# Tiny loads at the start of an attention and mixture-of-experts kernel, pair 1's loads, and a remade instruction order

## Chip, cores and metric

One core of one Trainium2 chip. The metric is the device time of one execution in microseconds (us); the median of three timed runs before the change is 482.71 us (482.61 to 484.01).

## What is computed

Attention of 4 batches with 8 heads, 768 positions and head size 64, in which each query sees the first 4 keys (the sinks) and the last 128; its output, 3072 tokens of 512 numbers, then goes through a mixture of 8 experts, of which each token takes one.

```python
keep = is_sink | in_window                      # window 128, 4 sinks
scores = where(keep, scale * q @ kT, -1e9)
a = softmax(scores); x = a @ v                  # x: 3072 tokens x 512
e_idx = argmax(x @ w_gate)                      # one expert for each token
eom = sigmoid(x @ w_output_gate)
for e in range(8):                              # tokens of expert e
    out[mask] = gate_w * eom[mask, e] * (relu(x[mask] @ w1[e]) @ w2[e])
```

## The kernel before

*Stages.* Attention goes through 16 pairs of heads (`pair(p)`). A pair loads q and k (for two heads), v for two pairs at once, and for each batch the sink values. Its scores come in three tiles of PSUM (L1481, `score(j)`, f32); DVE masks a tile and takes the row maximum (L1490 to L1497, `fold`), ACT scales the maxima (L1509) and takes the exponentials (L1502). PE transposes them (L1530), ACT copies them out (L1533), GpSimd (POOL) masks them (L568), and PE multiplies them by v in six steps, av0 to av5 (L1597), and by the sink values (L1621). The result is transposed, normed and written to DRAM (`xd`). After each four pairs tokens are routed to experts on DVE. Then 18 slots follow, each for one expert and up to 384 of its tokens: tokens are gathered, the expert's weights (4 MB) are loaded and most are split into a high and a low part (ACT L1150, DVE L1154), and PE runs two matrix products (L1299 and L1338; small slots L1312, L1245, L1260), with a ReLU between whose residue DVE makes (L1214). The scaled result is scattered to the output (L1193). The first four slots (`early`) are mixed into the last part of attention.

*The order.* Nothing here is in the order of the source. Every step is given to a `Plan` with `pl.op(engine, took, fn, r=, w=, at=, busy=, size=, behind=)`: what it reads and writes, the planned duration, how long it holds its engine, the bytes of a transfer (`size`), and other steps after which it comes (`behind`). `order()` then plays the program: at each turn it looks on each engine for the step that could start first, may take instead one that could start within a small margin (`NEAR`, for PE `AT["near"]`) and has a lower due time `at`, and takes the earliest of all engines. The due time is a priority and holds nothing back. `PIN` overwrites the due time of every step by its number. A transfer ends in the plan when all planned bytes before it and its own have passed at `RATE` (KB per us, in thousands), plus `LAND` ns; a step `behind` a transfer on its own engine waits in the plan for that planned landing. `behind` makes no wait on the chip: there each engine runs its instructions in the resulting order and waits for the data that they need, and a transfer is issued when its turn comes. For PE the plan also counts the fetching of its code: after each `CHUNK` of 256 instructions the next block must be there, and one block takes `FETCH` ns.

*The start.* PE warms up with matmuls on a constant (`begin`, L1399 and L1406) and, after pair 0's first score tile, with 14 fillers (`idle(1)`, L1399), each a step of its own that fills time while nothing else is ready. Loads go to the queues of SP (`nc.sync`) and ACT. For pair 0, q's first two blocks go to SP and k's first to ACT; k's and q's second pieces go to ACT behind a step that loads the table of exponentials. `small_loads` is one step on SP with five transfers: the gate weights `wgt` (L671, 64 KB), the two scalars `nsw_i` (L673, 8 bytes to each of 128 partitions), and the zero row of `xd` in two transfers (L674: 128 pieces of 16 bytes, L675). Pair 1's q and k (L1420) stand behind that step; v (L1443) and the sink values (L1449) stand behind nothing. `scalars` is a DVE step of eight small operations on `nsw_i` (L637 to L647); `wgt` is first used by `gate` after the fourth pair, the zero row by the first gather.

Of the kernel before, what the change touches and what calls it, by code (L numbers as in the profile page):

```python
# [19 lines left out]
P = 128  # L20
B, H, S, D = 4, 8, 768, 64
# [278 lines left out]
class Plan:  # L300

    LAG = {"PE": 260, "ACT": 60, "DVE": 80, "POOL": 55, "SP": 30, "X": 0}
    NEAR = {"PE": 60, "ACT": 60, "DVE": 60, "POOL": 100, "SP": 100, "X": 0}
    SWITCH = {"four": 170}
    RATE, LAND = 0.38, 2700
    CHUNK, FETCH = 256, 4600

    def __init__(self):
# [1649 lines left out]
```

## Time and profile before

| | before |
|---|---|
| timed runs, median (lowest to highest) | 482.71 us (482.61 to 484.01) |
| the profiled execution, its time | 486.86 us |
| its span, first to last instruction | 484.9 us |
| mean granted clock of PE | 0.992 |
| PE busy | 462.9 us (95%) |
| DVE, ACT, POOL busy | 330.7, 281.1, 151.9 us |
| moved by DMA | 116.74 MB, 241 GB/s |

The profile is one execution. Engines are PE (matmuls), PEld (PE's weight loads, which overlap matmuls), DVE, ACT, POOL; SPq, ACTq and POOLq are the instructions by which SP, ACT and POOL issue DMA transfers. PE's ends are modelled, so a busy PE may still run below its peak. A waiting engine's idle time is put down to what came last, by semaphore events; "issue" means that it waited for nothing that the profile shows. The granted clock is the share of PE's full clock that the throttle allowed.

### The profile page before, as it was taken

Reading aid. Unit: us, or ns where it says so; the run is one execution under the profiler, and the core shown is the slowest. Engines: PE = TensorE matmul, PEld = TensorE weight load, DVE = VectorE, ACT = ScalarE, POOL = GpSimd, SP = SyncE. Lnnn points to the kernel's source line nnn. Section 1 sums busy time; section 2 is a strip of 40 time slices with the busy share of each in tenths; the row PEclk is TensorE's granted clock in tenths of the full one; section 3 lists DMA queues with packets and bytes.
Section 4 is the critical chain, followed back from the end, with each engine's and each line's share of the span. In section 5 each row is a group of like instructions: output and inputs, shape, how many; then the busy total and the mean of one; then the engine's idle time right before and its main releaser. Section 6 shows DMA issues by size and latency. Waiting matters only on the chain.

```text
span 484.9 us, 13381 instructions
## 1 busy us (share of the span) xinstructions
PE 462.9 (95%) x5129; PEld 379.0 (78%) x5129; DVE 330.7 (68%) x713; ACT 281.1 (58%) x779; POOL 151.9 (31%) x270
## 2 busy tenths in 40 slices
PE   8899999998889999899999999999999999999992
PEld 4688786787679879698889999888866978968571
DVE  5675789889888989999999932605557677373200
ACT  4999879987877743466566222616536665462310
POOL 6435543837652133310532110311132121100211
PEclk9999999999989999999999999999999999999998
DMA  7665764675764775587997563855898978979980
GB/s 214 225 207 166 235 183 145 207 203 162 261 198 124 230 245 175 173 248 251 323 325 262 194 230 107 296 206 198 286 405 304 303 260 291 392 259 403 402 317 14
DMA packets 63147, 116.74 MB, mean 241 GB/s; under 512 B 8283, under 2 KB 27875, under 8 KB 63075
## 3 DMA queue, kind: packets, MB, share of 16 engines
q1 hardware_dynamic: 58226, 101.00, 62.3%
q0 software_dynamic: 4416, 14.14, 8.1%
q8 instruction: 42, 0.69, 0.6%
q10 hardware_dynamic: 432, 0.67, 0.5%
q14 instruction: 31, 0.25, 0.2%
HBM read 102.61 MB, written 13.17 MB: 239 GB/s over the span
## 4 chain that ended last, share of the span: by engine, by line
PE 66%; issue 14%; DVE 7%; ACT 4%; DMA 4%; POOL 3%; POOLq 0%; SPq 0%; ACTq 0%; DVEq 0%
PE d L1299 19%; PE d L1338 19%; PE d L1597 6%; PE d L1481 5%; PE tp L1530 4%; DMA k<-in_kx_dram 3%; PE d L1312 2%; ACT e L1502 2%; PE tp L1639 2%; PE tp L1175 2%; PE d L1621 2%; POOL out_dram L1193 2%; PE d L1260 1%; PE d L1245 1%; DVE nmx L1497 1%
## 5 line engine op out<-in xcount | busy, mean ns | idle before, releaser
L1502 ACT ACTIVATE e<-d,nmx 128x132 f32<-128x132 f32 x192 | 69.4, 377 | 1.4
L1193 POOL DMA_INDIRECT out_dram<-y,idx x21 | 22.6, 1077 | 127.4 <-ACT y L1190 115.2
L1211 ACT ACTIVATE hh<-d 128x512 fp32r<-128x512 f32 (+1 forms) x36 | 23.2, 644 | 50.8 <-PE d L1299 42.8
L1214 DVE SCALAR_TENSOR_TENSOR hl<-d,hh 128x512 fp32r<-128x512 f32 (+1 forms) x36 | 26.8, 745 | 32.7 <-ACT hh L1211 32.7
L1110 POOL DMA_INDIRECT xg<-xd,idx x21 | 24.2, 1150 | 76.2 <-PE tp L1175 33.9
L1481 PE MATMUL d<-k,q 64*64 64x128 f32 (+3 forms) x1088 | 44.3, 285 | 2.4 <-DMA k<-in_kx_dram 1.9
L1481 PEld LDWEIGHTS d<-k,q 64*64 64x64 f32 x1088 | 37.3, 135 | 10.2 <-issue 5.4
L568 POOL TENSOR_SCALAR_AFFINE_SELECT g<-f 128x512 f32<-128x512 f32 (+1 forms) x48 | 27.9, 582 | 54.2 <-ACT f L1533 48.0
L1597 PE MATMUL d<-f,v 64*64 64x128 f32 (+1 forms) x768 | 42.6, 252 | 1.2 <-issue 1.1
L1190 ACT ACTIVATE y<-d,sc 128x512 f32<-128x512 f32 (+2 forms) x29 | 17.9, 636 | 44.4 <-PE d L1338 22.9
L1502 ACT ACTIVATION_READ_ACCUMULATOR e<-d,nmx 128x1 f32 x192 | 40.5, 211 | 0.0
L1495 DVE COPY_PREDICATED d<-maskf,d 128x512 f32<-128x512 int32 (+1 forms) x48 | 29.0, 604 | 16.8 <-PE d L1481 10.9
L1597 PE MATMUL d<-g,v 64*64 64x128 f32 (+1 forms) x640 | 39.0, 253 | 1.0 <-ACT tick L1612 0.6
L1597 PEld LDWEIGHTS d<-f,v 64*64 64x64 f32 x768 | 34.6, 135 | 3.0 <-issue 2.6
L1497 DVE TENSOR_REDUCE nmx<-d 128x4 f32<-128x528 f32 x48 | 33.9, 707 | 1.6
L1597 PEld LDWEIGHTS d<-g,v 64*64 64x64 f32 x640 | 29.6, 135 | 4.1 <-issue 2.4
L1530 PE MATMUL tp<-ident,e 128*128 128x128 f32 x192 | 29.4, 281 | 2.4 <-ACT hlk L1567 2.0
L1533 ACT COPY f<-tp 128x512 f32<-128x512 f32 x48 | 28.0, 597 | 5.8 <-PE tp L1530 4.1
L1348 DVE TENSOR_SCALAR hr<-d 128x512 f32<-128x512 f32 (+1 forms) x12 | 7.7, 645 | 32.5 <-PE d L1245 18.2
L568 POOL TENSOR_SCALAR_AFFINE_SELECT f<-f 128x512 f32<-128x512 f32 (+1 forms) x48 | 28.8, 601 | 3.3
L1530 PEld LDWEIGHTS tp<-ident,e 128*128 128x128 f32 x192 | 21.1, 142 | 7.5 <-ACT e L1502 2.2
L795 POOL TENSOR_TENSOR rhs<-oh,ohj 128x512 bf16<-128x512 bf16 x12 | 15.4, 1306 | 14.3 <-DVE ohj L781 14.2
(488 smaller groups left out, 1434.1 us busy)
## 6 DMA issues: line engine op xcount, KB each, us to landing
raw<-in_w_dram SPq DMA_DIRECT2D x96, 512.0 KB
v<-in_vx_dram SPq DMA_DIRECT2D x16, 384.0 KB
xd<-x SPq DMA_DIRECT2D x16, 384.0 KB
k<-in_kx_dram SPq DMA_DIRECT2D x15, 396.0 KB
q<-in_qT_dram SPq DMA_DIRECT2D x15, 384.0 KB
wa2h<-in_w_dram SPq DMA_DIRECT2D x4, 512.0 KB
wa2l<-in_w_dram SPq DMA_DIRECT2D x4, 512.0 KB
wa1h<-in_w_dram SPq DMA_DIRECT2D x3, 512.0 KB
```

Of the source, the lines that this page charges most:

```text
L568: nc.gpsimd.affine_select(out=ap, in_=ap if src is None else src, pattern=pattern, compare_op=op, fill=fill, base=base, channel_multiplier=cm)
L1193: nc.gpsimd.indirect_dma_start(out=where, out_offset=bass.IndirectOffsetOnAxis(ap=ids(), axis=0), in_=p.get(yk)[:, 0:m], in_offset=None, b ...
L1214: nc.vector.scalar_tensor_tensor(out=p.get(hl)[:, :, 0:n], in0=p.get(ps)[:, :, 0:n], scalar=0.0, in1=p.get(hh)[:, :, 0:n].bitcast(F32), op ...
L1299: nc.tensor.matmul(out=p.get(ps)[:, j, 0:cols], lhsT=a, rhs=p.get(x)[:, d, 0:cols], start=d == 0 and i == 0, stop=d == ND - 1 and i == 2)
L1338: nc.tensor.matmul(out=p.get(ys[s][0])[:, ys[s][1], :], lhsT=h[a][:, s * P:(s + 1) * P], rhs=w[b_], start=f == 0 and i == 0, stop=f == NF ...
L1481: nc.tensor.matmul(out=to, lhsT=get(q)[r, qs], rhs=get(k)[r, c:c + n], start=True, stop=True)
L1495: nc.vector.copy_predicated(out=y[:, :, D + 4:3 * D + 4].rearrange("p n (u c) -> p n u c", u=2), mask=bc(maski[:, 1, 4:CW].rearrange("p (u ...
L1497: nc.vector.tensor_reduce(out=top(), in_=z[:, :, :, D:3 * D + 4], axis=AX.X, op=ALU.max, negate=True)
L1502: nc.scalar.activation(out=get(e)[:, t, a, :], in_=by_step()[:, a, i, D:3 * D + 4], func=AF.Exp, bias=get(nmx)[:, a, t:t + 1], scale=SCALE ...
L1530: nc.tensor.transpose(out=get(tp)[:, i, :], in_=get(e)[:, 2 * j + i // 2, i % 2, 4:CW], identity=ident)
L1533: nc.scalar.copy(out=get(f)[:, two].rearrange("p t a r -> p (t a) r"), in_=get(tp))
L1597: nc.tensor.matmul(out=o, lhsT=get(v)[rows_, kt, p % 2 * P + a * D:p % 2 * P + (a + 1) * D], rhs=get((f, g)[src == "g"])[rows_, kt, a, c0: ...
```

## The change

The step of small loads becomes three, with larger planned bytes. The second piece of pair 0's q goes to SP and no longer stands behind the table load. Pair 1's q and k, the first v and all sink values stand behind that piece in the plan. The plan's RATE, LAND and `near` change, pair 0's first two score tiles and the first five fillers get longer planned times, and the fetch of a block of code takes in the plan half the time of the queued bytes more (`CROWD`). `PIN` is new throughout: none of the 1898 due times stays, and 1900 stand there now, as there are two steps more. The diff shows only the first two lines of `PIN` on each side (numbers 10 and 11 are the second pieces of k and q; before, 12 is the small loads; after, 12 to 14 are `wgt`, the scalars and the zero row).

```diff
@@ -61,239 +61,242 @@
...
-    "xm": 12029, "st": 39215, "rt": 89574, "ft": 40462, "near": 54, "fu": 40316, "fv": -6834,
+    "xm": 12029, "st": 39215, "rt": 89574, "ft": 40462, "near": 0, "fu": 40316, "fv": -6834,
...
-    0: 170375, 1: 183025, 2: 234170, 3: 207036, 4: 209173, 5: 234024, 6: -57011, 7: -2769860, 8: -63555, 9: -60420,
-    10: -196814, 11: -213168, 12: -2613934, 13: 219356, 14: -2575280, 15: -2569229, 16: -2590146, 17: -2590366, 18:
...
+    0: 284048, 1: 304551, 2: 298792, 3: 283628, 4: 288927, 5: 291515, 6: 68786, 7: -5536575, 8: -481105, 9: -468029,
+    10: -471477, 11: -5305361, 12: -5303392, 13: -5283895, 14: -5290740, 15: 121475, 16: -4524559, 17: -5299047, 18:
...
@@ -302,8 +305,8 @@
     LAG = {"PE": 260, "ACT": 60, "DVE": 80, "POOL": 55, "SP": 30, "X": 0}
     NEAR = {"PE": 60, "ACT": 60, "DVE": 60, "POOL": 100, "SP": 100, "X": 0}
     SWITCH = {"four": 170}
-    RATE, LAND = 0.38, 2700
-    CHUNK, FETCH = 256, 4600
+    RATE, LAND = 0.37, 2900
+    CHUNK, FETCH, CROWD = 256, 4600, 0.5
 
     def __init__(self):
         self.ops, self.inst, self.fam = [], {}, {}
@@ -462,7 +465,8 @@
                 for edge in range((first // self.CHUNK + 1) * self.CHUNK, issued + 1, self.CHUNK):
                     at = t + late + o["busy"] * (edge - first) / o["count"]
                     late += max(0, ready_at - at)
-                    ready_at = max(at, ready_at) + self.FETCH
+                    ready_at = max(at, ready_at)
+                    ready_at += self.FETCH + self.CROWD * max(0, dma - ready_at)
             free[e] = t + late + o["busy"]
             if o["size"]:
                 dma = max(dma, t + o["busy"]) + o["size"] / self.RATE / 1000
@@ -667,15 +671,17 @@
         def small_loads():
             q = nc.sync
 
-            def load():
-                q.dma_start(out=wgt, in_=wgo)
+            def scalars_in():
                 for j, src in enumerate((nsink, window)):
                     q.dma_start(out=nsw_i[:, j, :], in_=src.bitcast(I32).partition_broadcast(P))
+
+            def row_0():
                 q.dma_start(out=xd[0, 0:DM].rearrange("(p c) -> p c", p=P), in_=tab[:, 0, 0, 0:4])
                 q.dma_start(out=xd[0:1, DM:XP], in_=tab[0:1, 0, 0, 0:XP - DM])
-            small = pl.op("SP", 2500, load, w=["wgt", "nsw_i", "xd0"], size=64, busy=2600, at=-1000000)
+            pl.op("SP", 2500, lambda: q.dma_start(out=wgt, in_=wgo), w=["wgt"], size=65536, busy=420, at=20000)
+            pl.op("SP", 2500, scalars_in, w=["nsw_i"], size=500000, busy=880, at=25000)
+            pl.op("SP", 2500, row_0, w=["xd0"], size=300000, busy=770, at=27000)
             pl.op("DVE", 1500, scalars, r=["nsw_i"], at=30000)
-            return small
 
         def rows(b):
             return xd[1 + b * S:1 + (b + 1) * S, :].rearrange("(t p) c -> p t c", p=P)
@@ -1425,12 +1431,12 @@
                 load(k, kx, 0, 2 * CW, "ACT", (0,), -2000000)
                 warmed = [pl.op("ACT", 1600, lambda: nc.scalar.activation(out=warm, in_=warm, func=AF.Exp), at=-1999999.5, busy=1500)]
                 paced["k"] = load(k, kx, 2 * CW, KW, "ACT", (1,), -1999999, warmed)
-                paced["q"] = load(q, qT, 2 * P, S, "ACT", (1,), -1999999, warmed)
-                paced["small"] = small_loads()
+                paced["q"] = load(q, qT, 2 * P, S, "SP", (1,), -1999999)
+                small_loads()
             for name, src, n in ((q, qT, S), (k, kx, KW))[:2 * (p > 0)]:
                 if p == 2:
                     touch([(name, 0), (name, 1)], lambda name=name: get(name), zeroed, at)
-                paced[name] = load(name, src, 0, n, "SP", (0, 1), (at, "load"), [paced[name[0], p - 1] if p > 1 else paced["small"]])
+                paced[name] = load(name, src, 0, n, "SP", (0, 1), (at, "load"), [paced[name[0], p - 1] if p > 1 else paced["q"]])
             v = ("v", p // 2)
             if p % 2 == 0:
                 new(pl, "v", [P, T, 2 * P], key=v)
@@ -1442,12 +1448,12 @@
                         c = slice(i * T // 2, (i + 1) * T // 2)
                         nc.sync.dma_start(out=get(v)[:, c], in_=vx[b, c, :, hp * P:(hp + 2) * P].rearrange("t p c -> p t c"))
                     paced["v", p, i] = pl.op("SP", 2000, load_v, w=[(v, i)], at=(at + i, "v"), size=P * 4 * S, busy=400,
-                                             behind=[paced["v", p - 2, i]] if p else ())
+                                             behind=[paced["v", p - 2, i]] if p else [paced["q"]])
             if hp == 0:
                 for i in range(2):
                     def sink_values(r=slice(i * D, i * D + 2 * SINK)):
                         nc.sync.dma_start(out=vsts[b % 2][r], in_=vs[b, 0:2 * SINK])
-                    pl.op("SP", 2000, sink_values, w=[(("vst", b % 2), i)], at=(at + i, "vs"), size=4 * 24 * 512, busy=400)
+                    pl.op("SP", 2000, sink_values, w=[(("vst", b % 2), i)], at=(at + i, "vs"), size=4 * 24 * 512, busy=400, behind=[paced["q"]])
                 new(pl, "lg", [P, T, 2 * E], key=("lg", b))
                 new(pl, "rs", [P, H // 2, 2, T], key=("rs", b))
             rs = ("rs", b)
@@ -1504,7 +1510,7 @@
                     return fn
 
                 reads = [x for n in (q, k) for x in ([(n, 0)], [(n, 0), (n, 1)] if n == k else [(n, 1)], [(n, 1)])[j]]
-                paced["s", p, j] = pl.op("PE", fn=mm, r=reads, w=[s], at=(at, "s%d" % j), behind=[paced["s", p - 1, j]] if p else (), **pe(724 if j else 505, "four", 48 if j else 40))
+                paced["s", p, j] = pl.op("PE", fn=mm, r=reads, w=[s], at=(at, "s%d" % j), behind=[paced["s", p - 1, j]] if p else (), **pe((724 if j else 505) if p or j == 2 else (1300 if j else 1000), "four", 48 if j else 40))
                 pl.op("DVE", fn=fold, w=[s, (nmx, j)], at=(at, "s%d" % j, "fold"), **took(1430 if j else 1800, 1346 if j else 1718))
                 pl.op("ACT", fn=lambda: nc.scalar.activation(out=top(), in_=top(), func=AF.Copy, scale=SCALE), r=[(nmx, j)], w=[(nmx, j)],
                       at=(at - 1, "s%d" % j, "exp"), **took(207, 107))
@@ -1516,7 +1522,8 @@
             if p == 0:
                 first = pl.inst["s", 0, 0]["users"][0]
                 for i in range(14):
-                    pl.op("PE", 216, lambda: idle(1), w=[spare], at=1000000 + i, mode="full", busy=216, soft=300, behind=[first], count=2)
+                    took_ = 216 if i > 4 else 427
+                    pl.op("PE", took_, lambda: idle(1), w=[spare], at=1000000 + i, mode="full", busy=took_, soft=300, behind=[first], count=2)
             f, g = new(pl, "f", [P, T, 2, P], key=("f", p)), new(pl, "g", [P, T - 1, 2, P], key=("g", p))
 
             def trans(j):
```

## Rows read from the trace of the kernel before

**Rows 1.** The page: busy time of PE, the instruction queue (packets, MB), loads of v.
```profile
PE 462.9 (95%) x5129; PEld 379.0 (78%) x5129; DVE 330.7 (68%) x713; ACT 281.1 (58%) x779; POOL 151.9 (31%) x270
...
q8 instruction: 42, 0.69, 0.6%
...
v<-in_vx_dram SPq DMA_DIRECT2D x16, 384.0 KB
```

**Rows 2.** Waits of PE over the whole span: us in total, times, longest.
```profile
PE d L1481 <- DMA k<-in_kx_dram: 1.9, 1, 1.9
PE d L1338 <- DVE hl L1214: 1.7, 1, 1.7
...
PE d L1597 <- issue: 1.4, 2, 1.1
```

**Rows 3.** Chain of work that ended last, first 30 us: start, duration, what.
```profile
1.71 5.37 DMA k<-in_kx_dram
...
7.83 5.28 DMA k<-in_kx_dram
```

**Rows 4.** Instructions in order of time, SP and POOL, first 8 us: start, duration.
```profile
1.28 0.42 SPq L671 DMA_DIRECT2D wgt<-in_wgo_dram  x1
...
4.59 0.53 POOL L1390 MEMSET vst<- 128x512 f32 x1
...
5.15 2.24 SPq L1449 DMA_DIRECT2D vst<-in_vs_dram  x2
...
7.43 0.36 SPq L1420 DMA_DIRECT2D q<-in_qT_dram  x1
```

**Rows 5.** Waits of SP, first 20 us: us in total, times, longest.
```profile
SPq L1449 <- DMA k<-in_kx_dram: 1.6, 1, 1.6
...
SPq L675 <- DMA k<-in_kx_dram: 0.5, 1, 0.5
```

**Rows 6.** Per stretch, busy us (count) of PE, PEld, DVE, ACT, POOL; clock, DMA share, GB/s.
```profile
6.00:7.00 1.00, 1.00 (x6) 0.46 (x5) 0.93 (x3) 0.00 (x0) 1.00 (x6) 1.00 0.30 22
10.00:11.00 1.00, 1.00 (x23) 0.68 (x25) 0.95 (x2) 0.58 (x1) 0.06 (x1) 1.00 0.99 375
```

**Rows 7.** Instructions in order of time, PE, DVE and ACT, 5 to 16 us.
```profile
5.84 2.76 PE L1399 MATMUL d<-ones 128*128 128x512 bf16 x12
...
7.78 0.17 DVE L637 CAST nswf<-nsw_i 128x4 f32<-128x4 int32 x1
...
9.54 0.70 DVE L1495 COPY_PREDICATED d<-maskf,d 128x512 f32<-128x512 int32 x1 [0.42 <-PE d L1481]
...
11.01 0.21 ACT L1509 ACTIVATE nmx<-nmx 128x4 f32<-128x4 f32 x1
...
15.72 0.21 ACT L1509 ACTIVATE nmx<-nmx 128x4 f32<-128x4 f32 x1 [0.31 <-DVE nmx L1497]
```

**Rows 8.** Busy us by stretch of 2 us, columns as in group 6.
```profile
132.00:134.00 2.00, 0.88 (x20) 0.70 (x18) 1.32 (x3) 1.33 (x6) 1.64 (x4) 1.00 1.05 342
134.00:136.00 2.00, 1.38 (x26) 1.14 (x28) 1.79 (x3) 0.83 (x6) 0.58 (x1) 0.89 0.75 241
136.00:138.00 2.00, 2.00 (x48) 2.00 (x44) 0.97 (x2) 2.00 (x10) 0.41 (x2) 0.50 0.83 248
138.00:140.00 2.00, 2.00 (x29) 1.64 (x27) 0.98 (x2) 0.83 (x2) 0.24 (x2) 0.75 0.83 264
```

**Rows 9.** Instructions of PE in order of time, 131 to 134 us.
```profile
131.83 0.28 PE L1597 MATMUL d<-g,v 64*64 64x64 f32 x2 [0.28 <-issue]
...
133.31 0.39 PE L1597 MATMUL d<-f,v 64*64 64x64 f32 x4 [1.12 <-issue]
```

**Rows 10.** Busy us by longer stretches, columns as in group 6.
```profile
100.00:110.00 10.00, 10.00 (x268) 8.33 (x270) 8.65 (x24) 8.26 (x34) 2.97 (x11) 1.00 0.87 225
200.00:230.00 30.00, 28.15 (x179) 24.59 (x178) 29.27 (x81) 17.30 (x21) 3.06 (x3) 1.00 0.81 247
```

**Rows 11.** The end of PE's work, instructions in order of time.
```profile
475.31 0.62 PE L1260 MATMUL d<-wc1l,hr 128*32 128x128 f32 x16
```

457 rows, old and new, of the table PIN are left out of this document.

## The prediction

> **What bounds the kernel now.** The page comes first. TensorE (PE) is busy 462.9 of 484.9 us [rows 1], so time can go only where PE idles, where its clock is low, or where it runs something useless. Its last matmuls start at 475.31 and take 0.62 [rows 11]; the span ends 9.0 us later, in a tail that no edit touches. The list of PE's waits is short [rows 2]: 1.9 us for the second pair's k, 1.7 for a ReLU residue on DVE, 1.4 under "issue" (it waited for nothing that is shown).
>
> Two places bear on this change. The first is the start. The chain of waits there runs over two transfers: k's second half, issued at 1.71, lands 5.37 us later, at 7.08, and lets SP go on; the second pair's k is issued at 7.83 and lands at 13.11 [rows 3], where that pair's scores begin. In SP's order the small loads stand right behind the first q piece, then v and the sink values, and pair 1's q goes out only at 7.43 [rows 4]. SP's waits say why: the thirteenth transfer issued (the second sink load) waited 1.6 us for the landing of the fifth (k's second half), the ninth (the second xd) 0.5 us for that of the first [rows 5]. That fits an issue which waits for the landing of the eighth transfer before it. From 6 to 7 us the DMA engines moved 22 GB/s at a busy share of 0.30, against 375 in a full stretch [rows 6], which I read as tiny pieces alone.
>
> The second place is at 130 us. PE stopped twice in the middle of one step of attention-times-v (L1597), for 0.28 and 1.12 us, by "issue" [rows 9], with the DMA engines 1.05 busy [rows 8]. A step in progress waits for no buffer, so I read this as instructions that came late. PE's code comes as 42 packets of the instruction queue, 0.69 MB, or 16.4 KB each [rows 1]. Right behind the stop the granted clock is 0.89, 0.50 and 0.75 in three stretches of 2 us [rows 8]: full is 2.4 GHz, 0.50 is 1.2.
>
> **The change part by part.** *Small loads.* One plan step of five transfers, which held SP 2.6 us in the plan, becomes three steps, and q's second piece moves from ACT's queue to SP's. I follow the plan's rule, not the due times: a free queue takes whatever can start. Pair 1's loads, v and the sink values now stand behind q's second piece, that is, behind its planned landing. Gate weights, row 0 and scalars stand behind nothing, so they fill the gap, and I expect SP's order q, q, wgt, xd, xd, nsw, nsw, pair 1's q, a sink load, pair 1's k, v. The tiny pieces leave the very head and yet stay ahead of pair 1. At 0.42 us an issue [rows 4] and a little between them, pair 1's q goes out near 4.4. The sink load needs its buffer zeroed, which ends at 5.12 [rows 4], so k goes out near 5.5 instead of 7.83. It also no longer queues behind two loads of v, 768 KB [rows 1], 2.1 us at 375 GB/s [rows 6]. Landing: at best 5.5 + 5.28 - 2.1 = 8.7; at worst the tiny pieces hold it and only the 2.1 are gained, 11.0. I take 10.2, nearer the worse end, as those pieces are still ahead of it in the same queue.
>
> *What is late next at the start.* Pair 1's scores can gain at most the 1.9 us that PE waited [rows 2]. But from 11.01 on ACT works almost without a break, and when pair 1's maxima reach it at 15.72 it has waited only 0.31 [rows 7]: alone, the earlier k is worth 0.3. More comes only if pair 0's second tile moves, which stands behind 12 filler matmuls of 0.23 us [rows 7]; by the plan's rule some 11 remain, 0.2 more. Against it stand the scalars on DVE, from 7.78 on, ahead of that tile's masking at 9.54 [rows 7]. They start as soon as the first tile's masking ends, so nothing covers a late landing of nsw. Its issues move from about 2 to about 4 us, a landing later by 0 to 1.8, of which 0.5 is offset by the two gains. The start lies between +1.3 and -1.9; I take -0.5, the two gains alone: by 4 us the pieces of q and k ahead of nsw are mostly moved, and of a delay the first 0.42 us falls into DVE's pause before 9.54 [rows 7].
>
> *q's second piece on SP.* ACT's queue loses one issue and sends k's second half some 0.4 us sooner; no tile waits for ACT so early, so 0 to -0.4, inside the start's bounds. The Trainium skill (DMA: Bandwidth & Descriptors, Queues, rings and completion order) says that each DMA engine takes turns between the queue rows of the issuing engines, a packet at a time. By that, tiny pieces on SP's row hardly delay k's half on ACT's, and taking them from ahead of it brings nothing. The 5.37 us that this half took [rows 3] speak against a full reading of it.
>
> *Fetches in the plan.* The plan now adds half of the backlog of queued bytes to each code fetch of 4.6 us; RATE, LAND, the first pair's matmul times, the fillers' and near (54 to 0) change its arithmetic alone. What they do is to remake the order: all due times differ. What this can repair is the stop at 130 us: 0.28 + 1.12 = 1.4 of waiting [rows 9] and 2 x (0.11 + 0.50 + 0.25) = 1.7 of PE time at low clock [rows 8], together 3.1. Behind it no other wait of PE in that stretch is over a microsecond. The Trainium skill (Runtime: NRT & Kernel Launch, Instruction fetch mechanics) says that the next block of code is fetched while one runs and that its cost is mostly hidden. By that this edit would be worth nothing; two stops inside one step speak against it here.
>
> *The rest of the order* has no row in the trace of before. At best it also removes the wait for the residue, 1.7 [rows 2]; at worst it makes a second stop with its low clock, 3.1. I charge 1.1, one long stop [rows 9], for a stop elsewhere in attention: from 100 to 110 us, for one, PE runs 268 matmuls and 270 weight loads with the DMA engines 0.87 busy [rows 10], and has no stop there now.
>
> Sum: -0.5 - 3.1 + 1.1 = -2.5 us. The profiled span of 484.9 becomes 482.4. That execution lasted 486.86, 4.15 over the median of the timed runs, 482.71; I apply the difference to the median: 480.2.
>
> **The rivals.** (1) *The gain is given back.* From 200 to 230 us DVE is busy 29.27 of 30 us [rows 10], and PE's 1.7 us for the residue are spent there. If DVE's splitting of weights holds PE, or a stop of the old size stands elsewhere, what remains is 0 to -1.0: 482.2. For it: that load. Against: DVE is less busy in attention, so its work can move forward with the rest.
>
> (2) *A second stop (slower).* The old one stays and another comes with its low clock: 482.71 - 0.5 + 3.1 = 485.3. Its place is a step of many short matmuls while weights are loaded; it decides as soon as a block of code comes later than the matmuls on hand last. For it: every due time is new, and 4.6 us is a guess. Against: the plan is now warned of just this.
>
> (3) *The small loads really go behind pair 1.* Then its k goes out near 2.2 and lands near 8, and scores and what follows gain the full 1.9 instead of 0.5: 478.8. Against: a free queue in this plan does not wait.
>
> (4) *Late code is not the cause.* In 42 fetches there is one place with stops that long [rows 1, 2], so something unseen may have made it, and it stays: 482.71 - 0.5 + 1.1 = 483.3. The page on instruction fetch of the Trainium skill, named above, would have it so.
>
> **How the numbers follow.** Forecast 0.44 and rival (3) 0.10: faster by more than 0.3%. Rivals (1) 0.14 and (4) 0.10: within 0.3%, 1.4 us, which is about what a measurement of this kernel can tell from no change. Rival (2) 0.22: slower. The likeliest time is 480.2. Low end: start -1.9, stop -3.1, residue -1.7, nothing charged, 476.0. High end: rival (2) with nothing gained at the start, 485.8. The forecast's own range is 476.0 to 481.2.
>
> **What would show it.** Pair 1's k issued near 5.5 and landing between 8.7 and 11; tiny pieces still ahead of it; pair 1's maxima on ACT 0.3 to 1 us before 15.72; no "issue" wait of a microsecond inside L1597, and no granted clock under 1.0 between 10 and 470 us; PE's last matmuls near 472.8. I am wrong if PE's waits in the middle grow by more than they lost, if another stretch runs at 0.50, or if pair 0's second tile is masked after 10.5 and ACT runs later from there on.

## The result, and the profile after

The changed kernel takes 478.49 us (median of 5 runs, 477.8 to 479.17), the kernel before beside it 482.71 (481.25 to 484.01): a ratio of 0.991, 95% interval 0.9885 to 0.9936, or 4.2 us less. On another chip it took 482.44 against 486.36, a ratio of 0.9904 (0.9881 to 0.9928). The forecast was 480.2, 2.5 us less.

The page of after, then PE's waits over the whole span (us in total, times, longest):

```profile
PE 459.8 (96%) x5129; PEld 376.8 (79%) x5129; DVE 328.0 (69%) x713; ACT 282.2 (59%) x779; POOL 154.3 (32%) x270
...
q8 instruction: 42, 0.69, 0.6%
```

```profile
PE d L1487 <- ACT e L1508: 1.8, 3, 1.0
PE d L1412 <- DVE ones L605: 1.5, 1, 1.5
PE d L1604 <- ACT e L1508: 0.8, 1, 0.8
```

Of the three waits of [rows 2], the one for k and the one in attention times v are gone, and 0.2 us is left of the one for hl. The count of matmuls and the 42 packets of code are those of [rows 1]; PE's busy time is 3.1 us less, 1.7 of it the low clock of [rows 8].

SP's first issues in order of time (start, duration), and the instructions of DVE and ACT that answer to [rows 7]:

```profile
0.81 0.89 SPq L1426 DMA_DIRECT2D q<-in_qT_dram  x2
1.75 0.44 SPq L681 DMA_DIRECT2D wgt<-in_wgo_dram  x1
2.23 0.43 SPq L679 DMA_DIRECT2D xd<-tab  x1
2.70 0.34 SPq L680 DMA_DIRECT2D xd<-tab  x1
3.09 0.37 SPq L676 DMA_DIRECT2D nsw_i<-in_nsink_dram  x1
3.63 0.34 SPq L676 DMA_DIRECT2D nsw_i<-in_window_dram  x1
4.02 0.48 SPq L1426 DMA_DIRECT2D q<-in_qT_dram  x1
6.01 0.30 SPq L1455 DMA_DIRECT2D vst<-in_vs_dram  x1
6.35 0.33 SPq L1426 DMA_DIRECT2D k<-in_kx_dram  x1
```

```profile
7.67 0.16 DVE L641 CAST nswf<-nsw_i 128x4 f32<-128x4 int32 x1
...
8.91 0.69 DVE L1501 COPY_PREDICATED d<-maskf,d 128x512 f32<-128x512 int32 x1
```

```profile
10.38 0.21 ACT L1515 ACTIVATE nmx<-nmx 128x4 f32<-128x4 f32 x1 [0.83 <-DVE nmx L1503]
...
14.80 0.21 ACT L1515 ACTIVATE nmx<-nmx 128x4 f32<-128x4 f32 x1
```

SP's order is the forecast one; pair 1's k goes out at 6.35 instead of 7.83 [rows 3] and lands at 9.67 instead of 13.11. Pair 1's maxima reach ACT at 14.80 instead of 15.72, 0.92 us earlier.

One profile of each kernel says little here: the profiled execution of before lay 4.15 us over the median of the timed ones, that of after 0.4. So both kernels were profiled twice. Worked out from the traces, the time in us at which PE begins the Nth of its 5129 matmuls, counted from 0 (the 3000th lies in the expert stage, and from there on both orders run nearly the same work):

```
kernel              3000th   3600th   last    3000th to 3600th   3600th to last
before               157.3    237.8   475.7        80.5               237.9
before_again         156.4    237.0   474.2        80.6               237.2
after                152.4    230.2   467.8        77.8               237.6
after_second         153.6    232.6   471.1        79.0               238.5
attention_new        153.3    233.9   470.8        80.6               236.9
attention_old        160.0    238.5   476.0        78.5               237.5
```

In these profiles the gain is made in two stages, up to 157 us and from there to 237 us; behind that nothing is gained. The last two rows belong to experiments below.

### The profile page after: what moved, and what is told of

Read it like the earlier page. It is cut to its first block, busy times and chain, and to the rows that moved or that the text cites. A ratio compares the mean times of both kernels' runs of the same rounds, so it can differ in the third digit from the quotient of the medians.

```text
span 477.1 us, 13389 instructions
## 1 busy us (share of the span) xinstructions
PE 459.8 (96%) x5129; PEld 376.8 (79%) x5129; DVE 328.0 (69%) x713; ACT 282.2 (59%) x779; POOL 154.3 (32%) x270
## 4 chain that ended last, share of the span: by engine, by line
PE 51%; issue 22%; DVE 12%; POOL 6%; ACT 5%; DMA 2%; POOLq 0%; DVEq 0%; ACTq 0%
PE d L1344 15%; PE d L1305 14%; PE d L1604 5%; PE d L1487 4%; POOL out_dram L1199 3%; PE tp L1537 3%; ACT e L1508 2%; POOL xg L1116 2%; PE tp L1646 2%; DMA xg<-xd,idx 2%; PE tp L1181 1%; PE d L1628 1%; PE d L1318 1%; DVE nmx L1503 1%; DVE d L1501 1%
## 5 line engine op out<-in xcount | busy, mean ns | idle before, releaser
L1199 POOL DMA_INDIRECT out_dram<-y,idx x21 | 21.0, 1000 | 122.8 <-ACT y L1196 101.3
L1116 POOL DMA_INDIRECT xg<-xd,idx x21 | 25.4, 1208 | 83.5 <-PE tp L1181 54.4
L1487 PEld LDWEIGHTS d<-k,q 64*64 64x64 f32 x1088 | 36.1, 133 | 10.3 <-issue 5.1
L1604 PE MATMUL d<-f,v 64*64 64x64 f32 (+1 forms) x768 | 41.1, 249 | 0.8 <-ACT e L1508 0.8
L1604 PE MATMUL d<-g,v 64*64 64x128 f32 (+1 forms) x640 | 37.5, 250 | 0.0
L572 POOL TENSOR_SCALAR_AFFINE_SELECT f<-f 128x512 f32<-128x512 f32 (+1 forms) x48 | 27.8, 578 | 3.3
L801 POOL TENSOR_TENSOR rhs<-oh,ohj 128x512 bf16<-128x512 bf16 x12 | 17.0, 1438 | 19.6 <-DVE perm L864 16.8
```

The costliest lines, as they stand in the source:

```text
L572: nc.gpsimd.affine_select(out=ap, in_=ap if src is None else src, pattern=pattern, compare_op=op, fill=fill, base=base, channel_multiplier=cm)
L1116: nc.gpsimd.indirect_dma_start(out=p.get(key), out_offset=None, in_=xd[0:n + 1, :], in_offset=bass.IndirectOffsetOnAxis(ap=ids(), axis=0))
L1199: nc.gpsimd.indirect_dma_start(out=where, out_offset=bass.IndirectOffsetOnAxis(ap=ids(), axis=0), in_=p.get(yk)[:, 0:m], in_offset=None, b ...
L1487: nc.tensor.matmul(out=to, lhsT=get(q)[r, qs], rhs=get(k)[r, c:c + n], start=True, stop=True)
L1604: nc.tensor.matmul(out=o, lhsT=get(v)[rows_, kt, p % 2 * P + a * D:p % 2 * P + (a + 1) * D], rhs=get((f, g)[src == "g"])[rows_, kt, a, c0: ...
```

## The experiments

In the diffs `seq` is the order that the plan found, and `put(ids, after)` moves the steps `ids` behind the step `after`.

**The same kernels again.** `before_again` is the kernel before, unchanged; `after_second` the changed one.

> The kernel before, unchanged, profiled a second time. Theory (code that comes late at 130 us is part of this order): the stop inside L1597 near 131 to 133 us and the low clock behind it are there again, span near 484.9. Rival (they belong to that one execution, whose 486.86 us was 4.15 over the median of the timed runs): no stop of a microsecond there, granted clock 1.0 throughout, span near 481.

> The changed kernel once more, on the same chip as the three above, with a second profile: 4.2 us faster than before (2.7 to 5.5); no stop over 0.4 us in the probability steps at 125-140 us, no wait of 1 us for hl near 195-200 us, the clock at 1.0 from 8 to 470 us. If the profile shows one of these stops, what I read from the first profile was chance.

before_again took 485.3 us, and its chip gave 485.46 as the median of 17 runs. PE stopped again in L1597 at 132.2 to 134.3 us, but the clock stayed at full there: the low clock behind the stop [rows 8] is not in every execution. after_second has a stop as well, in another step, which I had expected to be gone for good:

```profile
134.47 0.76 PE L1487 MATMUL d<-k,q 64*64 64x68 f32 x16 [1.08 <-issue]
```

I measure the stop from here on between the starts of neighbouring matmuls: the sum of all distances of 0.3 us and more inside a step of scores or of attention times v, 129 to 138 us. By idle time, as in [rows 9], it would be less, 1.4 us in before. It is 2.2 us in before, 2.1 in before_again, 0.5 in after, 1.7 in after_second (late code, below, is all of the 0.5 and 0.3 of the 1.7). What the first profile of after showed was half chance.

**The loads alone, and the order alone.** First before's order with the new loads, then the new order with the old loads; ids of the loads only.

```diff
-        for _, i in self.order():
+        put([7, 8, 9, 11, 12, 10, 78], 6)
+        put([17, 79, 15, 16], 4)
+        put([265, 264, 14], 5)
...
-                queue = nc.scalar if eng == "ACT" else nc.sync
+                queue = nc.scalar if eng == "ACT" and c0 != 2 * P else nc.sync
```

> The kernel before with its order of steps kept, but the transfers at the start as in the changed kernel: q's second piece on SP, then wgt, xd, xd, nsw, nsw, pair 1's q, one sink load, pair 1's k, v. Theory: pair 1's k lands 3 us earlier, but pair 1's scores gain little, since the 12 fillers and ACT stand: -0.3 to -0.6 us, ratio 0.999. Rival (the late k alone set the start): the full 1.9 us of PE's wait, ratio 0.996.

> The changed kernel with its order of steps kept, but the transfers at the start put back: q's second piece on ACT's queue, the five small transfers behind the first q piece, then v, sink values, and pair 1's q and k last. Theory: pair 1's k is issued near 7.8 and lands near 13 again, pair 1's first scores move from 12.3 to 13.3, and 0.5 to 0.9 us is lost: ratio to before 0.993. Rival (the loads carry most of the gain): ratio 0.997 or more. Rival (the earlier loads are hidden behind fillers and ACT): ratio as the changed kernel, 0.991.

before_new_loads: 485.04 against 485.46, ratio 0.9982 (0.9958 to 1.0006). after_old_loads: 481.27, ratio 0.9898 (0.9865 to 0.9931), as good as the whole change. So the loads are worth 0.9 us by the ratio, which cannot be told from nothing (the interval goes from 2.0 us faster to 0.3 slower), and the order is worth most of the gain. In the profile of after_old_loads PE does wait 2.6 us for pair 1's k:

```profile
PE d L1499 <- DMA k<-in_kx_dram: 2.6, 1, 2.6
```

but that execution, 484.12, was the longest of its seven.

**Twelve fillers.** The new order has eight filler matmuls ahead of pair 0's second tile; four were moved back.

```diff
+        put([43, 44, 45, 46], 42)
```

> The changed kernel with 12 instead of 8 fillers ahead of pair 0's second score tile, and 2 instead of 6 behind the third; nothing else moves. Theory: the second tile starts 4 x 0.23 = 0.9 us later, near 8.55; its masking on DVE, now at 8.91, starts near 9.5, and ACT's next maxima come 0.6 later: ratio to before 0.992 to 0.993. Rival (the fillers are idle time anyway, and the loads set the start): no change, 0.991.

481.84, ratio 0.9909 (0.9875 to 0.9943) to the same runs of before: no different from after. The fillers are not the gain.

**Is the stop late code behind queued loads?** In before_late_raw three weight loads of 512 KB, issued at 124 to 128 us, go behind the fifth, with their conversions.

```diff
+        put([1059, 1063, 1067], 1070)
+        put([1060, 1061, 1064, 1065, 1068, 1069], 1083)
```

> The order of before, with one move: the second to fourth weight load of the first early expert (512 KB each), which SP issued at 124-128 us, go behind the fifth (135 us), and their two conversions each on ACT and DVE with them. Nothing is left out. Theory (PE stopped in L1597 at 131-134 us because its code came behind these queued loads): the DMA share of 126-131 us falls well under 1, the three gaps of 0.5-0.6 us each (1.4 to 1.8 us together) go, so does the granted clock of 0.5 behind them; 1.0 to 2.5 us faster than before. Rival (code at that place is late whatever is queued, or the stop is not of code): the gaps stay, no change within 0.5 us. Second rival (the loads are missed later): the gaps go, but PE waits for weights or ACT near 140-150 us, and the end is not earlier.

The queue was light up to 130 us and the stop came all the same, 2.1 us in sum. Stretches of 2 us (busy us and count of PE, PEld, DVE, ACT, POOL; clock, DMA share, GB/s) and PE's instructions:

```profile
128.00:130.00 2.00, 2.00 (x61) 1.62 (x56) 1.83 (x10) 1.59 (x9) 1.07 (x4) 1.00 0.12 36
130.00:132.00 2.00, 1.85 (x37) 1.45 (x28) 0.85 (x2) 1.50 (x3) 1.70 (x2) 1.00 0.88 238
132.00:134.00 2.00, 1.05 (x14) 0.48 (x11) 0.63 (x1) 0.58 (x2) 1.03 (x2) 1.00 0.66 215
```

```profile
132.55 0.31 PE L1608 MATMUL d<-f,v 64*64 64x128 f32 x1 [0.29 <-issue]
...
133.32 0.28 PE L1608 MATMUL d<-g,v 64*64 64x64 f32 x2 [0.31 <-issue]
...
134.06 0.39 PE L1608 MATMUL d<-f,v 64*64 64x64 f32 x4 [0.40 <-issue]
```

As the first rival of that expectation has it, the stop stayed, so these loads are not its cause. The time says nothing on it: the kernel was slower, 492.87 against 486.36 (1.0113, 1.0078 to 1.0148), because PE then waited 5.9 us for an xl that stood behind the late conversions on DVE. Nor does the code packet fit. In the next experiment's profile the stop runs from 132.5 to 134.5, and the only packet of PE's code between 128 and 137 us starts at 134.3; in after_second it starts at 131.3, and the stop ends at 134.5 too. The one stop is over as soon as the packet starts, the other 3.2 us later. Nor can the instructions of the stop have been late: in all nine profiles with a stop, the packet with their code (see below on how packets and code go together) had ended 3.4 to 6.5 us before the stop began.

**Is the wait near 200 us on the path?** In before_hl_first the residue step for which PE waited 1.7 us [rows 2] goes ahead of a weight's low part on DVE.

```diff
+        put([1157, 1178], 1156)
```

> The order of before, with one move: on DVE the remainder step hl that PE waits for at 199.65 us (1.8 us) goes ahead of the low part of one weight (wc1l, 1.21 us; also ahead of wc2l and xl behind it). Nothing is left out. Theory (this wait is on the path to the end, and the new order's gain between 187 and 230 us is this wait): PE's wait for hl falls under 0.5 us, and the kernel is 1.3 to 2.2 us faster. Rival (DVE is the one that is late there, so the wait moves to the next thing it makes, wc or xl): the wait for hl goes and another of 1 to 2 us comes within 20 us; no change within 0.5 us.

487.36 against 486.36 (1.0012, 0.999 to 1.0033): nothing gained. The wait for hl is gone, and some 2 us later PE waits for the next thing that DVE makes (DVE first, then PE):

```profile
194.63 3.51 DVE L1014 TENSOR_SCALAR who<-key,top 128x8 f32<-128x8 f32 x1
198.06 0.68 DVE L1224 SCALAR_TENSOR_TENSOR hl<-d,hh 128x512 fp32r<-128x512 f32 x1
...
203.41 0.95 DVE L797 TENSOR_TENSOR ohrow<-io,jf 128x768 bf16<-128x768 f32 x1
```

```profile
204.43 0.83 PE L816 MATMUL tp<-rhs,ohrow 128*128 128x256 bf16 x6 [2.24 <-DVE ohrow L797]
```

DVE as a whole is late there. The first line may be the reason: a step on 8 columns lasted 3.51 us, and in before DVE works without a gap from there to the hl that PE waits for. With 0.23 us for that step, as elsewhere, hl would by estimate have come some 3 us earlier, ahead of PE's wait. No run changes that step alone, so this is not shown.

**All three moves at once** (new loads, late weight loads, hl first):

> The order of before with three moves at once: the change's loads at the start, the three weight loads late, hl ahead. Theory (the gain of 4.2 us is the sum of a small part at the start, the stop at 131 us and the wait at 200 us): 2.5 to 5 us faster than before, so within 1.5 us of the changed kernel. Rival (these places are not what sets the end; the new order gains by many small things): under 1.5 us.

492.33 against 486.36 (1.0116, 1.009 to 1.0141): PE waits 4.6 us for an xl behind the late conversions, which hides whatever the rest brings. So this run decides nothing between the two cases.

**The two halves of the order.** In attention_new the plan takes the new order (and loads) up to the first expert product and what is left in before's order; in attention_old it is the other way round. The choice of the next step becomes:

```diff
+        seq = [...]
...
-            best = None
-            for e, xs in ready.items():
...
+            t, i = next((start_of(i), i) for i in seq if i not in placed and not missing[i] and start_of(i) is not None)
```

> Half of the change: its loads and its order up to the first expert product (PE at about 145 us), then the steps that are left in the order of before. Nothing is left out. Theory (the gain lies in two places: 2 to 3 us by the end of attention, and 2 us by the wait near 200 us): 1.5 to 3 us faster than before, and DVE's wait near 200 us (1.8 to 2.2 us) is still there. Rival one (all of it is the attention half): 3.5 us or more faster. Rival two (all of it is the expert half): within 0.7 us.

> The other half: the loads and the order of before up to the first expert product (149 us), then the steps that are left in the order of the changed kernel. Nothing is left out. Theory: 1 to 2.5 us faster than before; the stop at 131 us is there, the wait of 1.8 us for hl near 200 us is not. Rival one (attention half alone): within 0.7 us, the wait near 200 us comes back in another place, since DVE gets its work as late as before. Rival two (expert half alone): 3.5 us or more faster.

attention_new: 481.48 against 482.20, ratio 0.998 (0.9963 to 0.9996), 0.7 us by the medians, 0.2 to 1.8 by the interval. attention_old: 488.73, ratio 1.0137 (1.0108 to 1.0166), 6.5 us slower. PE's longest waits in the one and in the other:

```profile
PE d L1435 <- DVE hl L1311: 1.8, 1, 1.8
```

```profile
PE tp L1621 <- ACT f L1624: 4.3, 2, 3.8
```

The halves don't add up to the whole. With the new attention alone the wait of 1.8 us for hl is still there. With the new expert order alone it is gone, and the stage from the 3000th to the 3600th matmul takes 78.5 us, near the new order's 77.8 and 79.0, not 80.5; but at the seam, at 145 us, PE loses 4 us for an f that ACT copies late. None of my three cases for that kernel had this.

**Is the stop tied to the gathers?** Every stop of a microsecond or more between 129 and 138 us, in either order, begins 1.7 to 3.4 us after the first of GpSimd's gathers (three in a row from about 129 us). The pauses of 0.3 to 0.8 us in the new order that begin ahead of it are something else (late code, below). In before_late_gather eight memsets push the gathers back by 5 us; in gathers_twice each of the first three is issued twice.

```diff
             def fn():
+                if first:
+                    for _ in range(8):
+                        nc.gpsimd.memset(p.get(key), 0.0)
                 nc.gpsimd.indirect_dma_start(out=p.get(key), ...
```

```diff
+                for _ in range(2 if first else 1):
                     nc.gpsimd.indirect_dma_start(out=p.get(key), ...
```

> The kernel before, with eight GpSimd memsets of the first gathered tile put ahead of the first of the four gathers (L1110, 128.7 to 134.6 us): the gathers start some 4 us later (the memsets' own length is what the profile will show), nothing else moves, nothing is left out. After the run with the late weight loads, two theories of PE's stops in L1597 at 131-134 us are left. One: the stop comes with the gathers (in every profile so far it begins 1.7 to 3.4 us after the first gather does, and before them no gather runs): then it moves by about the same 4 us, to 134-139 us, into another step, or goes where PE has less code there; none is left at 131-133.5 us. Two: it belongs to a place in PE's code (in the profiles of before's order it lies at PE's 5357th to 5398th instruction): then it stays in L1597 at the same instructions. The time itself is not the question; masks wait behind the gathers, so 0 to 4 us slower.

> The kernel before, with each of its first three gathers (L1110, from 128.7 us) issued twice into the same tile; nothing else moves and nothing is left out. PE's stops in L1597 at 131-134 us came in six of the seven profiles of before's order with the gathers at that time, 1.7 to 3.4 us after the first gather began, and in the seventh (the run with the old attention and the new expert order) not. Theory (the gathers' transfers starve PE's bursts of short matmuls): the stops are there and longer, 3 us or more in sum between 130 and 137 us, against 1.8 to 2.4 us. Rival (the stop is not of the gathers: another thing that differs between executions): at most 2.4 us, or none. Apart from that POOL's masks and packs come some 4 us later, which costs up to 5 us, as it did with the memsets.

before_late_gather, 487.29 in one run against 482.2: no stop at all (PE then waits 4.4 us for POOL's packs, which stand behind the memsets). GpSimd's first lines, then the stretches:

```profile
128.66 4.74 POOL L1113 MEMSET xg<- 128x528 f32 x8
133.98 1.25 POOL L1114 DMA_INDIRECT xg<-xd,idx_e  x1 [0.58 <-DVE wa0l L1158]
```

```profile
130.00:132.00 2.00, 2.00 (x58) 1.73 (x51) 1.93 (x4) 2.00 (x5) 1.83 (x4) 1.00 0.80 299
132.00:134.00 2.00, 2.00 (x56) 1.60 (x49) 2.00 (x4) 2.00 (x13) 1.30 (x4) 1.00 0.87 316
```

gathers_twice turned out another experiment than meant: the second gather into a tile waited for the first one's landing, so that one gather instead of three ran before 137 us, while the weight loads stayed where they are. It has no stop either, with the DMA engines as full as in before (0.96 and 1.01 busy from 130 to 134 us):

```profile
129.36 1.25 POOL L1112 DMA_INDIRECT xg<-xd,idx_e  x1 [0.86 <-DVE idx_e L839]
137.13 1.91 POOL L1112 DMA_INDIRECT xg<-xd,idx_e  x1 [6.53 <-DMA xg<-xd,idx_e]
```

(PE pauses there once, 0.4 us for DVE's x.) The time, 498.59 against 484.79, is that of POOL's late packs, 14.9 us of waiting.

So with before's attention: three gathers, with or without the weight loads, gave a stop of 1.7 to 2.2 us in six profiles of seven; one or none gave none in two of two. The seventh, attention_old, has three gathers and the loads and no stop; with the new attention three profiles of five have one of a microsecond or more. But the chip fits as well as the gathers do. On chips 12 and 5 all eight profiles have the stop, in either order; on chips 10 and 3, where the two runs with fewer gathers were made, none of four has it, attention_old and attention_new with their three gathers included. No profile on those two chips shows a stop that the fewer gathers could have removed, so the gathers are not shown to be the cause, and it stays open. Only that it belongs to a place in PE's code alone, the second theory, is out: the same instructions ran without a stop.

**Late code, in other places.** The traces show pauses of PE by "issue" ahead of the gathers too, for instance 0.97 us of idle time in before_late_gather:

```profile
111.44 0.82 PE L1485 MATMUL d<-k,q 64*64 64x196 f32 x14 [0.97 <-issue]
```

I take these for late code, by three things that go together at every one of them: the place, a packet and the pause. Counted over all of PE's instructions in the trace, each packet of 16 KB starts only after PE has passed its 193rd, 449th, 705th instruction and so on, every 256, and PE stops in front of the next such place until 1.2 to 1.6 us after that packet's end. In the fourteen profiles PE passes 308 such places from the 449th to the 5825th instruction. At 20 it pauses 0.3 us or more (between starts), and there the packet had ended at most 1.25 us ahead; at the other 288 it had ended 1.17 us or more ahead. In before_late_gather the packet ended at 109.88 and PE, held since 110.21 at instruction 4545, went on at 111.44. Sums of these pauses, and the stop without them, in us, one number for each profile (the chip of the first two is not on record):

```
chip           before's attention: late code; stop      new attention: late code; stop
before, after  0; 2.2                                   0.5; 0
12             0.7, 1.5; 2.1, 1.7                       0.3, 0; 1.4, 1.0
5              1.2, 1.5, 1.1; 1.8, 2.1, 1.8             0.3; 1.3
10             1.6, 1.5; 0, 0                           0.8; 0
3              2.2; 0
```

In the table's order: on chip 12 before_again and before_new_loads, then after_old_loads and after_12_fillers; on 5 before_hl_first, before_late_raw and before_three, then after_second; on 10 attention_old and before_late_gather, then attention_new; on 3 gathers_twice.

## Why the prediction was right, and where by luck

**Direction and range held; two terms of the sum were wrong and partly made up for each other, which was luck.**

*The start, -0.5.* The order of issues was right. The time of pair 1's k was not quite: I put it at 5.5, held by the zeroing of the sink buffer; the first sink load went out only at 6.01, and SP's list of waits names k's landing (1.4 us). The rule that I had read in [rows 5], an issue waits for the eighth transfer before it, held it (here it is the seventh, since two went out within 0.01 us), and I had not counted it through for the new sequence. The landing at 9.67 is inside the bounds all the same. The landing of nsw cost nothing: DVE starts on the scalars at 7.67, against 7.78, and no gap follows. The gain of 0.92 us in pair 1's maxima is inside the bounds, and so is the 0.9 us of the loads alone, if it is any.

*The stop, -3.1.* This step failed in its mechanism and in its size. Moving the loads did not move the stop, and the code of the stopped step had landed 3.4 us or more ahead, so it was not late code, and of that stop rival (4) was right. But late code does stop PE in this kernel, in places that the profile of before did not show: at 63 and 110 us in most profiles with before's attention, 0.4 to 1.5 us each. The Trainium skill (Runtime: NRT & Kernel Launch, Instruction fetch mechanics) calls the cost of a fetch mostly hidden; the traces agree at 288 places of 308 and not at the other 20. On each of chips 12, 5 and 10 the new order has 0.8 to 0.9 us less of these pauses (table above); in the profiles of before and after it has 0.5 more. Of the stop itself it has 0.6 to 0.7 us less on chips 12 and 5, and on chip 10 neither order has one. So the plan's dearer fetches may have paid as meant, only not where I looked; no run tells `CROWD` from the rest of the new order. The 1.7 us of low clock were in two of those seven profiles at that place, but they were real in another way: many of before's executions lose them somewhere. Their mean granted clock was 0.991, 0.990 and 0.992 on three chips, after's 0.995 and 0.995, with no execution under 0.994; one stretch of 3.41 us at half clock lowers the mean by 0.0035. On the three chips the executions of before with a clock of 0.993 and more were 0.4 to 0.7 us shorter than the median of all of them. Stop and clock together come to 1.0 to 1.1 us on chips 12 and 5, a third of the 3.1 that I booked, and late code adds 0.9.

*The rest of the order, +1.1.* Wrong in sign. I charged a new stop and counted the residue's 1.7 us as a bound only. The charge was of the right kind, since stops do move from step to step in the new order, but they are already counted above. What I left out, the stage around the residue, is the largest single piece: 80.5 us before, 77.8 and 79.0 after, 78.5 in attention_old, about -2.0. From the 3000th to the 3600th matmul PE is idle 2.2 to 2.7 us in the nine profiles with before's expert order, nearly all of it for DVE, and 0.2 to 0.9 us in the five with the new one. It is not the hl step by itself, as before_hl_first shows; I put it down to DVE's whole sequence there, which no run changes alone. PE's share of the stretch from 200 to 205 us, before and after:

```profile
200.00:205.00 5.00, 3.16 (x15) 2.02 (x14) 4.93 (x12) 1.05 (x1) 0.00 (x0) 1.00 0.77 218
```

```profile
200.00:205.00 5.00, 5.00 (x41) 4.83 (x40) 4.83 (x20) 3.31 (x5) 2.04 (x2) 1.00 0.83 204
```

Rival (1) rested on DVE's load in [rows 10]. DVE is hardly less busy after (29.01 of 30 us from 200 to 230), but PE waits less for it.

*The sum.* The attention half with the loads gave -0.7, stop and clock within it, on a chip whose median for before was 482.20; with the expert stage's -2.0 that makes -2.7. On the two chips where the whole change was timed it gave -4.2 and -3.9. The 1.2 to 1.5 us between can be the chip: the changed kernel was not timed on the chip of the halves (10), where before's median is 3 to 4 us lower than on chips 12 and 5 (482.2 against 485.5 and 486.4) and neither order has the stop. An estimate from the table, as if every pause reached the end: on chip 10 late code alone, -0.8, against the measured -0.7; on chip 5 late code -0.9, stop -0.6, clock -0.4 and the expert stage -2.0, together -3.9, as measured. That is one to three profiles for each number, so the fit may be luck, and no run shows that all of these pauses are on the path to the end.

*The signs that I named.* Right: SP's order, pair 1's maxima 0.3 to 1 us earlier, no granted clock under 1.0 between 10 and 470 us. Chance: no wait of a microsecond by "issue" in attention times v; the second profile has one, of 1.1 us, in the scores. Off: PE's last matmuls at 467.48, not 472.8, since I took that from the profile of before [rows 11], whose execution was 4.15 us over the median.

## What to carry to other kernels

Before a stop in a profile is booked as a gain, profile the same kernel once more, and an experiment and its control on the same chip: here half of the term was in one execution and not in the next, and the stop came on some chips and not on others. To call a stop late code, count PE's instructions: late code stopped it only at every 256th instruction, and until shortly after a packet's end. A wait is worth its length only if the engine that is waited for has nothing else late behind it; moving one step of a full engine moves the wait. And an order made by a plan is one thing: its halves, 0.7 us faster and 6.5 us slower alone, made 4.2 us together, so price a remade order by stages of the whole, with the engine that is full in each.

## What the runs showed of the hardware

*A step of DVE can stand still behind GpSimd.* In before, the comparison on 8 columns at 194.97 lasted 3.51 us, against 0.23 in after, as long as GpSimd's three products beside it; in after the products take 5.57 us instead, and DVE's steps lengthen less (1.21 to 2.07 and 0.95 to 1.80). Before, then after, each GpSimd's line and DVE's:

```profile
195.37 3.07 POOL L795 TENSOR_TENSOR rhs<-oh,ohj 128x512 bf16<-128x512 bf16 x3
```

```profile
194.97 3.51 DVE L1004 TENSOR_SCALAR who<-key,top 128x8 f32<-128x8 f32 x1
```

```profile
190.13 5.57 POOL L801 TENSOR_TENSOR rhs<-oh,ohj 128x512 bf16<-128x512 bf16 x3
```

```profile
189.35 0.23 DVE L1010 TENSOR_SCALAR who<-key,top 128x8 f32<-128x8 f32 x1
...
191.01 2.07 DVE L1160 TENSOR_TENSOR wc3l<-raw,wc3h 128x1024 fp32r<-128x1024 f32 x1
193.00 1.80 DVE L793 TENSOR_TENSOR ohrow<-io,jf 128x768 bf16<-128x768 f32 x1
```

The lengths 3.5 and 3.1 stand in the profiles of before_again, before_hl_first and attention_new as well, 2.1 and 5.6 in after_second and attention_old: they go with the order of the expert stage. The Trainium skill (SBUF — State Buffer, SBUF: two separate sides) says that DVE (in a two-port mode, or with two inputs in SBUF) and GpSimd share one pair of ports, that whoever starts first holds it for the whole instruction, and that "the other fully blocks". The trace agrees that here DVE waited in full, with one thing more: the DVE step was held through all three products, not through one. Its record begins 0.4 us ahead of GpSimd's, whose spans are rough, so who came first is not to be read there. In before these 3.3 us end 1.8 us ahead of PE's wait for hl, with DVE busy throughout in between.

*Low clock comes and goes.* By the mean clock of each execution, stretches of 3.41 us at 1.2 GHz fell in about half of before's (28 of 51 under 0.993) and in none of after's eleven. Between 10 and 470 us the longest distance between two starts of matmuls is 1.1 and 1.3 us in the two profiles of after, 2.1 and 2.6 in those of before. In the fourteen profiles all eleven low stretches ahead of the end begin while PE waits or within a microsecond of the end of a wait or stop. But the same wait does not always bring one: that for hl, 1.7 to 1.8 us in seven profiles, was followed by one in two of them.

*PE stops when a block of its code lands late.* The place, the packet's end and the pause go together at all 20 pauses (above). The stop at 129 to 138 us, in bursts of short matmuls (7 to 13 ns apart), is another one, of open cause. Nor are long matmuls free of such pauses: from 234 to 246 us, during or behind a later run of gathers, PE pauses 0.6 to 1.2 us by "issue" (between starts) in L1299's product in before, before_late_raw, before_three and after_second, and not in front of a new block.
